# Batch 0 of a linear-attention kernel: nine tokens of k and v to a partition, one load queue, and v cast on chip

## The chip, the cores and the metric

The kernel runs on one NeuronCore of a Trainium2 chip. The metric is the device time of one execution in microseconds (us), as the median of several runs. A profiled execution gives a trace of every instruction of the five engines (PE is TensorE, DVE is VectorE, ACT is ScalarE, POOL is GpSimd, SP is SyncE) and of every DMA transfer.

## The reference

```python
# q, k, v: (8 batches, 8 heads, 576 tokens, 64), float32
q_s = softmax(q, axis=-1)                      # over the 64 features
k_s = softmax(k, axis=2)                       # over the 576 tokens
kv  = einsum('bhsd,bhse->bhde', k_s, v)
att = einsum('bhsd,bhde->bhse', q_s, kv)       # -> x: (8, 576, 512)
xn  = (x - mean(x)) / sqrt(var(x) + 1e-6) * g_ln
out = x + relu(xn @ w_ch1) @ w_ch2             # 512 -> 2048 -> 512
```

## The kernel before, in words

One pass over eight batches and a ninth group, C9, that holds the last 64 tokens of all batches. For each batch the kernel takes exponentials of q and k, forms k'v for each pair of heads, divides by k's sums, multiplies q's exponentials with it, normalises the rows, and runs the two large products with w1 and w2. TensorE's matmuls are written in a fixed order (`run` weaves a list of side steps into the list of matmuls by a position), and each engine works through its own instructions strictly in the order of the program. DMAs are issued in program order too: those of the queue SP by SyncE, those of GpSimd's queue by GpSimd between its computing instructions.

Everything that the change touches is the prologue, `first_batch()`, and its helpers, and one entry in the list of side steps of batch 0:

- q of batch 0 comes in four tokens to a partition (`T = 4`); k and v of batch 0 come in `T0 = 6` tokens to a partition, so that 576 tokens lie on `P0 = 96` partitions. Tokens 0 and 1 of q, then k in four pieces of two heads, are issued on SP's queue (L970, L980). A small copy on GpSimd (`gate`, L1004) waits for q's landing and holds back what GpSimd issues behind it: v in three pieces, cast to bf16 by the DMA itself (L1006), tokens 2 and 3 of q (L970), the first 512 columns of w1 in two halves (L1013), the other three blocks of w1 (L99), the first blocks of w2 (L103), and then the loads of batch 1.
- `warm(17)` and `warm(6)` are matmuls on zeros that keep TensorE busy (L867).
- `exp_qt` (L220) and `norm_q` (L274, L923) treat one token group of q; `eq_pT` (L928, L934 or L930) transposes it on TensorE and copies it from PSUM.
- `exp_k0` (L293) takes the exponentials of two heads of k. `z0_mm` (L306) sums them over the tokens by matmuls with a column of ones, `recip_z` (L314) takes the reciprocals.
- `kv0_mm` (L321, L322) multiplies a pair of heads with both heads of v as one 128 by 128 product, scales it and masks the two off-diagonal blocks (`diag`) with VectorE, which also sums the rows. From the sums ScalarE or VectorE writes a 128 by 128 weight `mbc` (L327, L331), which subtracts the mean.
- `xT_mm` (L342) forms the transposed, mean-free rows of x for tokens 0 and 1 from `kv_sb` and `mbc`, in two PSUM banks of two column blocks each; `xT_out` (L351 on VectorE for blocks 0 and 1, L353 on ScalarE for 2 and 3) scales them by the gain.
- The matmuls with w1 for batch 0 are L520 (`mm1_part`), first over m 0 to 3 for tokens 0 and 1. Between them `q0_rest(t)` does `z_q` (L940) and `po_mm` (L414) of tokens 2 and 3, `x_fast` and `x_normed` (L464, L475) finish these rows, and `xn_pT` transposes them (L928, L932).

The line that ends the first load group and the lines that order GpSimd's queue:

```python
        nc.gpsimd.tensor_copy(out=gate, in_=q0[:, 1, 0, 0:4])
        for h0, hn in ((0, 4), (4, 2), (6, 2)):
            nc.gpsimd.dma_start(
                v0[0:P0, h0 : h0 + hn].rearrange("p h t d -> p h (t d)"), src0(v, h0, hn)
            )
        for t in range(2, T):
            load_q0(t, 1, nc.gpsimd)
```

Of the kernel before, what the change touches and what calls it, by code (L numbers as in the profile page):

```python
# [12 lines left out]
FP32 = mybir.dt.float32  # L13
BF16 = mybir.dt.bfloat16
# [6 lines left out]
def kernel(  # L21
# [16 lines left out]
    nc = tc.nc  # L38
# [33 lines left out]
    ident = const.tile([P, P], BF16)  # L72
    eps_ln = const.tile([P, 1], FP32)
    gate = const.tile([P, 4], FP32)
    ones = const.tile([P, 1], BF16)
    junk = const.tile([P, P], BF16)
    scrap = const.tile([P, 512], BF16)
    bones = const.tile([P, 2], BF16)
    ones_w = const.tile([P, P], BF16)
    diag = const.tile([P, P], FP32)  # L80
    mbc = const.tile([P, NP, P], BF16)
# [204 lines left out]

    kvbox = {}

    def exp_k0(j):
        hs = slice(2 * j, 2 * j + 2)  # L290
        if j == 0:
            eks[0] = raw.tile([P, T0, H, D], BF16, tag="kt", name="ek0", bufs=1)
        nc.scalar.activation(  # L293
            eks[0][0:P0, :, hs, :].rearrange("p t h d -> p h t d"), raws[0][0][0:P0, hs], AF.Exp
        )

    def k0_mm(j, t):
        hs = slice(2 * j, 2 * j + 2)
        return eks[0][0:P0, t, hs, :], raws["v0"][0:P0, hs, t, :], P

    def z0_mm(j):

        if j == 0:
            kvbox["z0"] = mm_ps.tile([P, NP], FP32, tag="m", name="z0")
        for t in range(T0):
            nc.tensor.matmul(  # L306
                kvbox["z0"][:, j : j + 1], k0_mm(j, t)[0], ones[0:P0],
                start=(j == 0 and t == 0), stop=(t == T0 - 1), skip_group_check=True,
            )

    def recip_z():
        kvbox["rz"] = sml.tile([P, NP], FP32, tag="rzk", name="rzk")
        kvbox["sum"] = sml.tile([P, NP], FP32, tag="lnv", name="kvs")
        nc.vector.reciprocal(kvbox["rz"], kvbox["z0"])  # L314

    def kv0_mm(j):
        pool, tag = (att_ps, "a") if j < 2 else (mm_ps, "m")
        pkv = pool.tile([P, P], FP32, tag=tag, name="pkv")
        for t in range(T0):
            lhsT, rhs, w = k0_mm(j, t)  # L320
            nc.tensor.matmul(pkv[:, 0:w], lhsT, rhs, start=(t == 0), stop=(t == T0 - 1))  # L321
        nc.vector.scalar_tensor_tensor(  # L322
            kv_sb[:, 0, j, :], in0=pkv, scalar=kvbox["rz"][:, j : j + 1], in1=diag,
            op0=ALU.mult, op1=ALU.mult, accum_out=kvbox["sum"][:, j : j + 1],
        )
        if j < NP - 1:
            nc.scalar.activation(  # L327
                mbc[:, j], ones_w, AF.Copy, scale=kvbox["sum"][:, j : j + 1]
            )
        else:  # L330
            nc.vector.tensor_scalar_mul(  # L331
                out=mbc[:, j], in0=ones_w, scalar1=kvbox["sum"][:, j : j + 1]
            )

    def xT_mm(j, kh):

        if j == 0:
            pobox["T", kh] = mm_ps.tile([P, 2, 2, P], FP32, tag="m", name="pxT")
        ops = [(kv_sb[:, 0, j, :], j % 2)] if j // 2 == kh else []
        ops += [(mbc[:, j], i) for i in range(2)]  # L340
        for n, (lhsT, i) in enumerate(ops):
            nc.tensor.matmul(  # L342
                pobox["T", kh][:, i], lhsT, eqTs[0][:, 0:2, j, :],
                start=(j == 0 and n == 0), stop=(j == NP - 1 and n >= len(ops) - 2),
                skip_group_check=True,
            )

    def xT_out(i):
        dst, src = xnTs[0][:, 0:2, i, :], pobox["T", i // 2][:, i % 2]
        if i < 2:  # L350
# [4 lines left out]
    halves = (slice(0, 64), slice(64, P))  # L355

    def kv_pairs(b, ts=range(T + 1)):

# [501 lines left out]
        for _, fn in side[done:]:  # L860
            fn()

    def warm(n):

        w = mm_ps.tile([P, 4, P], FP32, tag="m", name="warm")
        for _ in range(n):
            nc.tensor.matmul(w, junk, junk[:, 0:4].to_broadcast([P, 4, P]), start=True, stop=True)  # L867

    def prep_fast(b):

# [74 lines left out]
    def eq_pT(c, t, eng):  # L945
        pe_T(eqTs[c], eqs[c][0][:, t].rearrange("p h d -> p (h d)"), t, eng)
# [10 lines left out]
    def first_batch():  # L957

        nc.scalar.preload_act_table_set("natural_log_exp_and_others")
        raws[0] = (  # L960
            mlp.tile([P, H, T0, D], FP32, tag="hT", name="kt0", bufs=1), None,
            raw.tile([P, H, T, D], FP32, tag="qt", name="qt"),
        )
        k0, _, q0 = raws[0]
        v0 = mlp.tile([P, H, T0, D], BF16, tag="hs", name="v0", bufs=1)
        raws["v0"] = v0

        def load_q0(t, tn, eng):
            ts = slice(t, t + tn)
            eng.dma_start(  # L970
                q0[:, :, ts],
                q[0, :, 0:SM, :].rearrange("h (p t) d -> p h t d", t=T)[:, :, ts],
            )

        def src0(x, h0, hn):
            return x[0, h0 : h0 + hn].rearrange("h (p t) d -> p h (t d)", t=T0)

        load_q0(0, 2, nc.sync)
        for h0 in range(0, H, 2):
            nc.sync.dma_start(  # L980
                k0[0:P0, h0 : h0 + 2].rearrange("p h t d -> p h (t d)"), src0(k, h0, 2)
            )
        raws["g"] = outp.tile([KO1, P], FP32, tag="ot", name="g_rows")
        nc.scalar.dma_start(
            raws["g"], bass.AP(moe_g_ln.tensor, moe_g_ln.offset, [[P, KO1], [1, P]])
        )
        nc.vector.memset(junk, 0.0)
        nc.vector.memset(eps_ln, 1e-6)
        nc.vector.memset(ones, 1.0)
# [3 lines left out]
        nc.vector.memset(ones_w, -1.0 / DM)  # L993
        nc.vector.memset(diag, 0.0)
        for ps in halves:
            nc.vector.memset(diag[ps, ps], 1.0)
        nc.vector.memset(kv_sb[:, 1:B], 0.0)
# [7 lines left out]
        for h0, hn in ((0, 4), (4, 2), (6, 2)):  # L1005
            nc.gpsimd.dma_start(  # L1006
                v0[0:P0, h0 : h0 + hn].rearrange("p h t d -> p h (t d)"), src0(v, h0, hn)
            )
        for t in range(2, T):
            load_q0(t, 1, nc.gpsimd)  # L1010
        for kh in range(2):
            ks = slice(2 * kh, 2 * kh + 2)
            nc.gpsimd.dma_start(w1_sb[:, ks, 0:512], w1_src[:, ks, 0:512])  # L1013
        for nb in range(1, 4):
            load_w1(nb)
        load_w2(0)
        load_w2(1)

        new_eq(0)
        start_x(0)  # L1020
        warm(17)
        for t in range(2):
            exp_qt(0, t)
            norm_q(0, t)
        eq_pT(0, 0, nc.vector)
        warm(6)
        eq_pT(0, 1, nc.vector)
        for j in range(NP):
            exp_k0(j)
            z0_mm(j)  # L1030
            if j == NP - 2:
                g_columns()
        recip_z()
        kv0_mm(0)
        kv0_mm(1)
        kv0_mm(2)
        xT_mm(0, 0)
        kv0_mm(3)
        exp_qt(0, 2)
        exp_qt(0, 3)  # L1040
        xT_mm(1, 0)
        xT_mm(2, 0)
        xT_mm(0, 1)
        xT_mm(3, 0)
        xT_out(0)
        xT_out(1)
        eq_pT(0, 2, nc.scalar)
        xT_mm(1, 1)
        xT_mm(2, 1)
        eq_pT(0, 3, nc.vector)  # L1050
        xT_mm(3, 1)
        xT_out(2)
        xT_out(3)

    def q0_rest(t):
        z_q(0, t)
# [35 lines left out]
    with tc.manual_schedule(  # L1092
# [11 lines left out]
        def po_x(c, t):  # L1104
            for i in range(NP):
# [85 lines left out]
```

## Time and profile before

| | |
|---|---|
| Median of 3 runs | 262.19 us (261.9 to 262.19) |
| Profiled execution: its own time | 262.09 us |
| Profiled execution: span of its instructions | 260.3 us, granted clock 1.000 |
| Outside the span | 1.8 us |
| TensorE busy | 253.9 us (98%) |
| VectorE, ScalarE, GpSimd busy | 223.1, 177.5, 103.2 us |
| DMA moved | 45.04 MB, mean 173 GB/s |

Times in the prologue are microseconds from the start of the span. In the views of the trace each line names an engine, the line of the kernel, the operation, and "output tile <- input tiles"; PEld is the loading of a matmul's weights, which overlaps the matmuls. A line number can be that of a helper: L520 is every matmul with w1 of batch 0 and some of batch 1. The chain of waits follows, from the last instruction backwards, what released each piece of work.

### The profile page before, as it was taken

The page shows a single profiled execution, that of the slowest core. Times are in us where ns is not written, and L with a number is a line of the kernel's source. Part 1 is how long each engine was busy: PE and PEld are TensorE (multiplying, and loading weights), DVE is VectorE, ACT ScalarE, POOL GpSimd, SP SyncE. Part 2 cuts the span into 40 slices and gives each one's busy share as a digit, 9 for nine tenths or more (in the row PEclk, how much of TensorE's full clock was granted, in tenths as well). Part 3 has the DMA queues.
Part 4 walks back from the last instruction along what each step waited for, and adds up shares of the span by engine and source line. Part 5 has one row for each costly group of instructions (what it writes and reads, how often), then busy time and mean ns, then how long its engine had stood idle before and what let it go on. Part 6 is the DMA issues. An engine that isn't in the chain of part 4 may idle for free.

```text
span 260.3 us, 7286 instructions
## 1 busy us (share of the span) xinstructions
PE 253.9 (98%) x2885; PEld 215.6 (83%) x2885; DVE 223.1 (86%) x542; ACT 177.5 (68%) x348; POOL 103.2 (40%) x160
## 2 busy tenths in 40 slices
PE   8899999999999999999999999999999999999993
PEld 3689755788888888888888988888889888888883
DVE  6768996989989998899889988998899889957873
ACT  4747790997988685888588858885788386647400
POOL 3953247410299409800980098008200900190000
PEclk9999999999999999999999999999999999999999
DMA  6999999988699995999699859989902630422014
GB/s 198 257 203 208 354 221 332 257 169 308 118 122 321 268 120 107 300 247 107 142 300 235 86 135 304 232 89 161 279 0 50 142 137 1 77 71 99 3 40 121
DMA packets 82618, 45.04 MB, mean 173 GB/s; under 512 B 58196, under 2 KB 79192, under 8 KB 82584
## 3 DMA queue, kind: packets, MB, share of 16 engines
q0 software_dynamic: 32464, 21.76, 45.8%
q1 hardware_dynamic: 49488, 22.29, 36.8%
q10 hardware_dynamic: 632, 0.53, 0.7%
q8 instruction: 22, 0.36, 0.6%
q14 instruction: 12, 0.10, 0.1%
HBM read 36.70 MB, written 9.44 MB: 177 GB/s over the span
## 4 chain that ended last, share of the span: by engine, by line
PE 92%; DMA 4%; POOL 2%; DVE 0%; issue 0%
PE ba L604 21%; PE bx L762 20%; PE bb L762 10%; PE ph L520 8%; PE bb L604 6%; PE be L604 5%; PE bc L604 5%; PE pc L556 5%; PE bc L762 5%; DMA w_raw<-in_moe_w_ch_dram 3%; PE pkv L371 2%; DMA qt<-in_q_dram 2%; PE po L403 2%; PE ptr L928 1%; PE po L414 1%; POOL v L1006 1%
## 5 line engine op out<-in xcount | busy, mean ns | idle before, releaser
L604 PEld LDWEIGHTS <-hs 128*128 128x128 bf16 x512 | 49.6, 98 | 6.0
L269 POOL TENSOR_TENSOR tq<-xnT 128x256 bf16<-128x256 bf16 x30 | 20.1, 671 | 85.3 <-PE bc L604 73.9
L762 PEld LDWEIGHTS <-w_raw 128*128 128x128 bf16 x480 | 46.7, 98 | 5.5
L604 PEld LDWEIGHTS <-hT 128*128 128x128 bf16 x392 | 37.6, 98 | 4.2
L762 PEld LDWEIGHTS <-w1g 128*128 128x128 bf16 x360 | 34.7, 98 | 4.3 <-issue 0.2
L762 PE MATMUL bx<-tq,w_raw 128*128 128x256 bf16 x240 | 31.3, 273 | 0.0
L604 PE MATMUL ba<-w_q,hs 128*128 128x256 bf16 x256 | 30.6, 273 | 0.0
L786 ACT COPY bc<-bx 128x512 f32<-128x512 f32 x30 | 16.7, 596 | 19.1 <-PE bx L762 19.1
L427 ACT ACTIVATE scrap<-x,mv 128x512 bf16<-128x512 bf16 x32 | 23.1, 723 | 4.6 <-DVE mv L457 4.4
L793 DVE TENSOR_TENSOR bb<-bx,s 128x512 f32<-128x512 f32 x30 | 19.5, 694 | 7.2 <-ACT s L790 4.5
L804 ACT ACTIVATE hT<-bb 128x512 bf16<-128x512 f32 x30 | 16.3, 595 | 9.3 <-PE bb L762 9.3
L804 ACT ACTIVATE hT<-bc 128x512 bf16<-128x512 f32 x30 | 16.5, 595 | 8.5 <-PE bc L762 8.5
L796 DVE TENSOR_TENSOR hT<-bx,s 128x512 bf16<-128x512 f32 x30 | 19.3, 684 | 3.2 <-PE bx L762 3.1
L587 DVE TENSOR_TENSOR hs<-hT 128x1024 bf16<-128x1024 bf16 x32 | 21.4, 672 | 0.5 <-ACT hT L804 0.5
L229 DVE TENSOR_REDUCE zq<-eq 128x16 f32<-128x1024 bf16 (+1 forms) x20 | 20.7, 1049 | 0.5 <-ACT eq L220 0.5
L269 POOL TENSOR_TENSOR tq<-xnT,tq 128x256 bf16<-128x256 bf16 x30 | 20.0, 669 | 1.1
L449 DVE SCALAR_TENSOR_TENSOR x<-po,rq 128x256 bf16<-128x256 f32 x48 | 17.5, 420 | 1.7 <-PE po L403 1.7
L790 ACT COPY s<-bb 128x512 f32<-128x512 f32 x30 | 16.6, 622 | 0.0
L804 ACT ACTIVATE hT<-bx 128x512 bf16<-128x512 f32 x30 | 16.4, 610 | 0.0
L762 PE MATMUL bx<-xnT,w1g 128*128 128x256 bf16 x120 | 16.2, 273 | 0.0
L762 PE MATMUL bx<-tq,w1g 128*128 128x256 bf16 x120 | 15.9, 272 | 0.0
L762 PE MATMUL bc<-xnT,w1g 128*128 128x256 bf16 x120 | 15.8, 273 | 0.0
(157 smaller groups left out, 535.0 us busy)
## 6 DMA issues: line engine op xcount, KB each, us to landing
out_dram<-ot POOLq DMA_DIRECT2D x30, 256.0 KB, 4.4
kt<-in_k_dram SPq DMA_DIRECT2D x5, 1024.0 KB, 11.6
qt<-in_q_dram SPq DMA_DIRECT2D x4, 1024.0 KB, 9.9
qt<-in_q_dram POOLq DMA_DIRECT2D x2, 1024.0 KB, 12.7
kt<-in_k_dram POOLq DMA_DIRECT2D x2, 1024.0 KB, 14.5
vm<-in_v_dram POOLq DMA_DIRECT2D x16, 128.0 KB, 12.4
qt<-in_q_dram SPq DMA_DIRECT2D x3, 512.0 KB, 5.7
w_raw<-in_moe_w_ch_dram POOLq DMA_DIRECT2D x3, 512.0 KB, 10.5
```

The costliest lines, as they stand in the source:

```text
L229: nc.vector.reduce_sum(eqs[c][1][:, ts], eqs[c][0][:, ts], axis=AX.X)
L269: nc.gpsimd.tensor_tensor(out=dst[:, t], in0=x[:, t], in1=y[:, t], op=ALU.subtract)
L427: nc.scalar.activation(scrap, x[:, t], AF.Square, bias=mv[:, t, 0:1], scale=-float(DM), accum_out=mv[:, t, 1:2],)
L449: nc.vector.scalar_tensor_tensor(x[:, t].rearrange("p (i two d) -> p i two d", two=2, d=D)[:, :, half], in0=pobox[c, t][half], scalar=1.0, ...
L520: nc.tensor.matmul(ph[:, m % 2, at : at + tn], (w1g if c else w1_sb)[:, ko, m * P : (m + 1) * P], xnTs[c][:, t0 : t0 + tn, ko, :], start=( ...
L587: nc.vector.tensor_tensor(out=dst, in0=x, in1=y, op=op)
L604: nc.tensor.matmul(hbox[bank][:, t, cs], lhsT, rhs[:, cs], start=first and (own or t == 0) and k == 0, stop=k == KH - 1, skip_group_check= ...
L762: nc.tensor.matmul(dst[:, q], lhsT, rhs, start=first and q == 0 and ko == 0, stop=ko == 1, skip_group_check=True)
L786: nc.scalar.copy(at[g, "c"], at[g, "x"])
L793: nc.vector.tensor_tensor(out=at[g, "b"], in0=at[g, "x"], in1=at[g, "s"], op=ALU.add)
L796: nc.vector.tensor_tensor(out=h_out(g, 1, 1), in0=at[g, "x"], in1=at[g, "s"], op=ALU.add)
L804: nc.scalar.activation(h_out(g, odd, half), at[g, name], AF.Relu)
```

## The change

- `T0` becomes 9. k and v of batch 0 lie on 128 partitions: 64 token groups of one head on partitions 0 to 63, the other head of the pair on 64 to 127, 2304 bytes in a row.
- SP's queue issues, in this order: q's tokens 0 and 1, four pieces of k, four pieces of v in fp32, and tokens 2 and 3 of q in four pieces of two heads. GpSimd's queue no longer carries v or q of batch 0. Its `gate` now waits for the last piece of k; behind it come the two halves of w1's first block, with two casts of v between them, blocks 1 and 2 of w1, and, at the end of the prologue, the copy `kv0_copy`, block 3 of w1 and the first blocks of w2.
- v is cast to bf16 by ScalarE (piece 0, parts of 2 and 3), GpSimd (piece 1, part of 3) and VectorE (part of 2), into a tile with a 65th column of ones, so that the sums of k's exponentials come out of the k'v product. `z0_mm` and `recip_z` go.
- k'v is formed for each head by itself: nine matmuls of 64 by 64 weights on partitions 0 to 63 and nine on 64 to 127, alternating, into a PSUM bank for each pair of heads. For two pairs at a time VectorE takes the reciprocals and scales one pair, ScalarE scales the other, both with row sums, and VectorE makes the mean column `kvm`; it is used as a weight by broadcasting it to 128 columns. GpSimd copies the result into `kv_sb`, which VectorE clears entirely beforehand.
- Each of the four column blocks of the transposed x has a PSUM bank of its own: 16 matmuls with the mean, 8 with the 64-row halves of `kvc`. `xT_out` uses VectorE for blocks 0 and 2, ScalarE for 1 and 3.
- The warming matmuls become three with fp32 and four with bf16 operands, and later one and two.
- The transposes of token 3 (`eq_pT(0, 3)`, with ScalarE's copy) move behind the first w1 matmuls, and `q0_rest(3)` one position back.

```diff
-    T0 = 6
-    P0 = S // T0
+    T0 = 9
...
+    def cast_v0(j, eng, ts=slice(0, T0)):
+        dst, src = raws["v0"][:, j, ts, 0:D], raws["v32"][:, j, ts]
...
+    def kv0_mm(j):
+        kvbox["kv0", j] = pkv = att_ps.tile([P, VW], FP32, tag="a", name="pkv")
+        for t in range(T0):
+            for ps in halves:
+                nc.tensor.matmul(
+                    pkv[ps], eks[0][ps, j, t], raws["v0"][ps, j, t],
+                    start=(t == 0), stop=(t == T0 - 1), skip_group_check=True,
+                )
+    def kv0_out(pair):
...
+        a, b = 2 * pair, 2 * pair + 1
+        nc.vector.reciprocal(rz[1], kvbox["kv0", b][:, D:])
+        nc.vector.reciprocal(rz[0], kvbox["kv0", a][:, D:])
+        nc.scalar.activation(
+            kvc[:, b], kvbox["kv0", b][:, 0:D], AF.Copy, scale=rz[1], accum_out=total[1]
+        )
+        nc.vector.scalar_tensor_tensor(
+            kvc[:, a], in0=kvbox["kv0", a][:, 0:D], scalar=rz[0], in1=ones_f,
+            op0=ALU.mult, op1=ALU.mult, accum_out=total[0],
+        )
+        js = slice(a, b + 1)
+        nc.vector.tensor_scalar_mul(
+            out=kvm[:, js], in0=kvbox["sum"][:, js], scalar1=-1.0 / DM
+        )
+    def kv0_copy():
+        for ps in halves:
+            nc.gpsimd.tensor_copy(out=kv_sb[ps, 0, :, ps], in_=kvc[ps])
...
-        load_q0(0, 2, nc.sync)
-        for h0 in range(0, H, 2):
-            nc.sync.dma_start(
-                k0[0:P0, h0 : h0 + 2].rearrange("p h t d -> p h (t d)"), src0(k, h0, 2)
-            )
+        load_q0(0, 2)
+        for dst, x in ((k0, k), (v32, v)):
+            for j in range(NP):
+                load_pair(dst, x, j)
+        for h0 in range(0, H, 2):
+            load_q0(2, 2, slice(h0, h0 + 2))
...
-        nc.gpsimd.tensor_copy(out=gate, in_=q0[:, 1, 0, 0:4])
...
+        nc.gpsimd.tensor_copy(out=gate, in_=k0[:, NP - 1, 0, 0:4])
+        load_w1_half(0)
+        cast_v0(1, nc.gpsimd)
+        load_w1_half(1)
+        cast_v0(3, nc.gpsimd, slice(0, 5))
+        for nb in range(1, 3):
+            load_w1(nb)
...
-        warm(17)
+        warm(3, junk_f)
+        warm(4)
         for t in range(2):
             exp_qt(0, t)
             norm_q(0, t)
         eq_pT(0, 0, nc.vector)
-        warm(6)
-        eq_pT(0, 1, nc.vector)
         for j in range(NP):
             exp_k0(j)
...
+        warm(1, junk_f)
+        warm(2)
+        eq_pT(0, 1, nc.vector)
+        cast_v0(0, nc.scalar)
+        g_columns()
         kv0_mm(0)
+        cast_v0(2, nc.vector, slice(0, 4))
+        cast_v0(2, nc.scalar, slice(4, T0))
         kv0_mm(1)
+        cast_v0(3, nc.scalar, slice(5, T0))
+        kv0_out(0)
         kv0_mm(2)
-        xT_mm(0, 0)
         kv0_mm(3)
+        for j in range(2):
+            xT_mean(j, 0)
+            xT_mean(j, 1)
+            xT_kv(j)
+        kv0_out(1)
         exp_qt(0, 2)
...
+        xT_mean(2, 0)
+        xT_mean(3, 0)
         xT_out(0)
         xT_out(1)
-        eq_pT(0, 2, nc.scalar)
...
+        xT_kv(2)
+        xT_kv(3)
+        eq_pT(0, 2, nc.vector)
+        xT_mean(2, 1)
+        xT_mean(3, 1)
+        exp_qt(0, 3)
         xT_out(2)
         xT_out(3)
+        kv0_copy()
+        load_w1(3)
+        load_w2(0)
+        load_w2(1)
...
-                (4, lambda: q0_rest(3)),
+                (3, lambda: eq_pT(0, 3, nc.scalar)),
+                (5, lambda: q0_rest(3)),
```

More of the change, by code (lines that the diff above doesn't have):

```diff
@@ L74 @@
     gate = const.tile([P, 4], FP32)
-    ones = const.tile([P, 1], BF16)
     junk = const.tile([P, P], BF16)
+    junk_f = const.tile([P, P], FP32)
     scrap = const.tile([P, 512], BF16)
     bones = const.tile([P, 2], BF16)
-    ones_w = const.tile([P, P], BF16)
-    diag = const.tile([P, P], FP32)
-    mbc = const.tile([P, NP, P], BF16)
+    ones_f = const.tile([P, D], FP32)
+    kvm = const.tile([P, NP], BF16)
+    kvc = const.tile([P, NP, D], BF16)
     g_one = const.tile([P, KO1], FP32)
@@ new lines, in kv0_mm @@
+    def kv0_mm(j):
[7 more added lines that the diff above has]
+    def kv0_out(pair):
+        if pair == 0:
+            kvbox["rz"] = sml.tile([P, NP], FP32, tag="rzk", name="rzk")
+            kvbox["sum"] = sml.tile([P, NP], FP32, tag="lnv", name="kvs")
+        rz, total = [
+            [kvbox[n][:, j : j + 1] for j in (2 * pair, 2 * pair + 1)] for n in ("rz", "sum")
+        ]
+        a, b = 2 * pair, 2 * pair + 1
+        nc.vector.reciprocal(rz[1], kvbox["kv0", b][:, D:])
+        nc.vector.reciprocal(rz[0], kvbox["kv0", a][:, D:])
@@ L311, in recip_z @@
[L311 to L333, printed above, removed]
@@ L345, in xT_mm, with xT_kv @@
                 skip_group_check=True,
             )
+    def xT_kv(j):
+        for ps in halves:
+            nc.tensor.matmul(
+                pobox["T", j][ps], kvc[ps, j], eqTs[0][ps, 0:2, j, :],
+                start=False, stop=False, skip_group_check=True,
+            )
     def xT_out(i):
-        dst, src = xnTs[0][:, 0:2, i, :], pobox["T", i // 2][:, i % 2]
-        if i < 2:
+        dst, src = xnTs[0][:, 0:2, i, :], pobox["T", i]
+        if i % 2 == 0:
             nc.vector.tensor_scalar_mul(out=dst, in0=src, scalar1=g_one[:, i : i + 1])
@@ L986, in first_batch @@
         )
+        nc.vector.memset(junk_f, 0.0)
         nc.vector.memset(junk, 0.0)
         nc.vector.memset(eps_ln, 1e-6)
-        nc.vector.memset(ones, 1.0)
         nc.vector.memset(bones, 0.0)
@@ L992, in first_batch @@
         nc.vector.memset(bones[64:P, 1:2], 1.0)
[L993 to L997, printed above, removed]
+        nc.vector.memset(ones_f, 1.0)
+        nc.vector.memset(raws["v0"][:, :, :, D:], 1.0)
+        nc.vector.memset(kv_sb, 0.0)
         nc.vector.memset(vr, 0.0)
```

85 lines of the change are left out of this document (28 added, 57 removed).

## The prediction

> **What bounds the kernel now.** I read the page first, then TensorE's waits, the chain of waits, the stages and the order of time of the first 20 us.
>
> The page's first table and TensorE's waits over the whole span (who waited for whom: total us, times, longest):
>
> ```profile
> PE 253.9 (98%) x2885; PEld 215.6 (83%) x2885; DVE 223.1 (86%) x542; ACT 177.5 (68%) x348; POOL 103.2 (40%) x160
> ...
> PE ptr L928 <- DVE eq L923: 1.0, 1, 1.0
> PE ph L520 <- DMA w_raw<-in_moe_w_ch_dram: 0.4, 1, 0.4
> ```
>
> TensorE is never idle long after 7.4 us; the last wait it has before its final matmul is 0.4 us for the second half of w1. So what the prologue costs is decided by when TensorE reaches the unbroken stretch of w1 matmuls, and everything behind it shifts with that moment. The chain of waits of the first 20 us shows the place (start us, us, what):
>
> ```profile
> 9.82 6.86 DMA w_raw<-in_moe_w_ch_dram
> 16.68 0.05 issue
> 16.72 0.61 PE ph L520 x4
> ...
> 18.44 0.95 PE ph L520 x16
> 19.39 0.34 PE ptr L928 x4
> 19.74 0.33 PE ph L520 x3
> ```
>
> The landing at 16.68 releases TensorE. The unbroken stretch (m 4 to 7, tokens 0 and 1) begins with a matmul at 19.57, shown here as 19.74. That is my mark. The order of time (start, length, engine, line, operation) gives its inputs:
>
> ```profile
> 6.11 0.82 ACT L293 ACTIVATE ek<-kt 96x768 bf16<-96x768 f32 x1
> 8.16 1.82 ACT L293 ACTIVATE ek<-kt 96x768 bf16<-96x768 f32 x2 [0.19 <-DMA kt<-in_k_dram]
> 11.83 0.50 PE L321 MATMUL pkv<-v,ek 96*128 96x128 bf16 x6
> 12.44 1.40 ACT L220 ACTIVATE eq<-qt 128x512 bf16<-128x512 f32 x2
> 14.62 0.60 PE L520 MATMUL ph<-xnT,w_raw 128*128 128x256 bf16 x4
> ```
>
> The trace's landing records put q at 5.03, k at 6.06, 7.11, 8.14 and 9.12, v at 10.18, 10.92 and 11.72, q's tokens 2 and 3 at 12.42 and 13.19, the w1 halves at 14.37 and 16.68. The last v releases the last k'v product, and 2.90 us after it (14.62) the first w1 matmul starts. The stages (us, busy by engine, granted clock, DMA share, GB/s) show that the DMA engines are full throughout:
>
> ```profile
> 3.00:4.50 1.50, 1.50 (x5) 0.56 (x4) 1.33 (x2) 0.00 (x0) 0.00 (x0) 1.00 1.13 357
> 5.50:7.50 2.00, 1.01 (x7) 0.28 (x5) 1.83 (x5) 1.80 (x4) 2.00 (x4) 1.00 1.08 285
> 8.50:10.50 2.00, 2.00 (x39) 1.59 (x38) 1.52 (x6) 1.35 (x2) 2.00 (x3) 1.00 1.31 200
> ```
>
> 357 GB/s is mostly q on 128 partitions, 285 is k on 96, 200 (as written, so 400 as read) is v being cast.
>
> **The change, part by part.** I walk to the mark in the new order; all times are us from the span's start.
>
> *k and v on 128 partitions.* An engine ends q at 4.50 at the latest. k's 1536-byte records then take 87 ns in the median on 96 partitions, but 65 ns (23.6 bytes/ns) in the first piece. q's 512 bytes take 27 ns with a pitch near 24 ns, and a 1024-byte load of a later batch 46 ns, on 128 partitions. For 2304 bytes I take 23.7 bytes/ns, 97 ns, since all clean rows on 128 partitions lie near it; the ends are 90 ns (the rate of 410 GB/s that q of batch 1 reaches) and 130 ns (k's 87 ns scaled by size). Each piece puts 8 records on an engine, 0.78 us, and k's last landing (9.12) trails its last record (8.43) by 0.69. So k lands at 6.0, 6.7, 7.5 and 8.3 (0.8 earlier at the end) and v at 9.1, 9.8, 10.6 and 11.37, against 11.72: 0.35 gained. At the ends v's last is 10.95 or 13.5.
>
> *Exponentials and casts.* ScalarE's line through 512 (0.62) and 768 elements (0.84) gives 0.68 for 576; the last exponential of k ends at 8.95 instead of 9.98, which no longer matters as v comes later. The casts of v are new work. Pieces 0 to 2 hide under the next piece's landing. Piece 3 does not: ScalarE's 4 tokens (256 elements) cost 0.40, GpSimd's 5 tokens about 0.46 by its copy of 1024 elements in 1.17; should its fp32 read cost double, 0.3 more.
>
> *GpSimd's order.* The gate now waits for k's last piece (8.3, was q's 5.03). Behind it are queued: w1's first half (issue 0.77), the cast of v's piece 1 (waits 9.8), w1's second half (issued 10.6 to 11.3), the cast of piece 3 (11.4 to 11.9), w1's blocks 1 and 2, the copy into kv_sb (waits for the last kvc), then w1 block 3 and w2. TensorE waits for that copy only at po of token 2, near 15.2; it is done by 14.4. The w1 issues stay ahead of the data, since the queue already holds over 2 us of transfers.
>
> *From v's last landing (11.37) to the first w1 matmul.* ScalarE's cast ends at +0.41, kvc(1) with its accumulator read at +0.68 (0.21 for the read, L485's), the mean column on VectorE at +0.85, TensorE starts xT at +0.90. VectorE's reciprocals of two pairs (0.18 each, by L314) and its product are done by then; the second pair's reach kvm at +1.80, under the first pair's matmuls. The removed z matmuls (24) and their reciprocal were not what ended last, and I credit nothing. xT is then bound by TensorE: 16 mean matmuls at 0.109, 4 pairs at 0.109 (two 64-row halves side by side, as L371 runs its halves), 4 transposes 0.23: 1.74 + 0.44 + 0.23 = 2.41. Together +3.31, so the first w1 matmul at 14.68. Unpaired halves would add 0.44.
>
> *From there to the mark.* Before, TensorE's work from 14.62 on is 8 matmuls, two z and po groups, and after the 0.4 wait 3.0 us up to 19.57: 4.5 net of the wait. The new order adds the transposes of token 3 (0.23) and a wait: z of token 3 is queued behind ScalarE's copy (0.58) of those transposes, about 0.38. Saved is the wait for w1, which should land near 15.6, with need at 16.1. The sum is 5.03 (rounding in the pitches), the mark 19.71, and +0.14 against 19.57.
>
> *q's tokens 2 and 3, the decisive cost.* They move from GpSimd's queue to the end of SP's, behind v: 64 records of 512 bytes an engine at 24 ns, 1.56 us. Alone, they end at 12.3 and land at 12.96. exp_qt(0, 2) then needs 0.62, the transposes, 4 mean matmuls: landing + 1.38 is the earliest first w1 matmul, and up to a landing of 13.3 nothing is late. Queued on ScalarE behind that exponential are xT_out(1) and exp_qt(0, 3); on TensorE, behind the transposes, the second half of xT and all of w1. But w1's first half is issued at 8.5, and its records (98 ns, pitch 82 ns) come on the other queue. In the trace v, issued from 5.20, shows its first record at 7.72, when the first engine has just finished k (7.71): what was already queued on SP went first. Later in this trace loads of SP and of GpSimd go one for one (59 and 60 records per 0.25 us at 113.5). I take it that most of q goes first and the last 8 to 12 records an engine alternate with w1: 8 to 12 times 82 ns, 0.65 to 1.0 us. The landing is then 13.6 to 13.9, the first w1 matmul 15.0 to 15.3, and the mark +0.5 to +0.75. I take +0.6.
>
> A page bears on this: the Trainium skill, DMA: Bandwidth & Descriptors, "Queues, rings and completion order", says each engine takes the queues with work in turn, packet by packet. By that rule w1 enters at once, and the rival below is the result; the trace agrees at 113.5 us and not at 7.7.
>
> *The rest.* Three fp32 and four bf16 warming matmuls replace 17; the only clue to their length is the 0.43 us of a cold bf16 one. Anything up to 1.3 us too long hides under the 1.0 us wait at 6.4 to 7.4 and the gap before k'v; a saving buys nothing. VectorE's set-up writes lose ones_w and diag (0.17 + 0.17 + 0.28) and gain 0.22 on kv_sb and some 0.4 for junk_f, ones_f and v's ones: it must be free at 5.66, and is. kv0 in 18 small matmuls costs under 0.4 a pair, one after each cast. Behind the mark nothing changes; data is 0.2 to 0.6 earlier, TensorE later, so no wait for w1 or w2 arises.
>
> The sum: 262.09 (profiled; the median shown is 262.19) + 0.6 is 262.7, or 262.8 against the median.
>
> **The rivals.**
>
> 1. *Faster: landings and a shorter chain* (0.29). If records of 2304 bytes go at 90 ns, v's last lands at 10.95 and q's at 12.4, both early enough: the first w1 matmul comes at 14.26 (-0.28 at the mark). If the copy behind z of token 3 also stays hidden, another 0.38 goes: 261.4 to 261.9. It decides as soon as the first w1 matmul is before about 14.0 or that wait is absent. For it: k's first piece at full rate. Against it: it needs both.
>
> 2. *Slower: w1 alternates with all of q's tokens 2 and 3* (0.20). If w1 enters at 11.0 (2.5 us after its issue, as v did), each of q's records waits for one of w1's: 16 get through before, the other 48 take 32 turns of 106 ns beside both halves of w1 and 16 more beside block 1, to 16.1; landing 16.8, the first w1 matmul 18.2, the mark +3.6: 265.7. It costs anything from a landing after 13.3 on; with half of it, 263.9.
>
> 3. *Slower: large records are no quicker on 128 partitions* (0.08). At 130 ns v's last lands at 13.5: +2.2, 264.4.
>
> 4. *TensorE falls back to half clock* (0.03). Between 9.3 and 12.3 it now works some 1.2 us. Half speed over 3.4 us, the time the clock needed at the start (matmuls of 0.43 until 4.3), costs 1.7: 264.5. The trace has no such fall after an idle 1.0 us.
>
> The forecast keeps 0.40: first w1 matmul between 14.7 and 15.6, 262.2 to 263.2.
>
> **How the numbers follow.** 0.2% (0.52 us) is about what a measurement of this kernel can tell from no change. The forecast is split about evenly by that bound, 0.18 within and 0.22 beyond. Rival 1 gives 0.25 beyond and 0.04 within; rivals 2 to 4 give 0.29 beyond on the slow side and 0.02 within. So: faster 0.25, same 0.18 + 0.04 + 0.02 = 0.24, slower 0.22 + 0.29 = 0.51. The range leaves out a tenth at each end: rival 1's better part and the worse half of rival 2, 261.3 to 265.2.
>
> **What would show it.** Right: k's last landing near 8.3, v's near 11.4, q's tokens 2 and 3 near 13.7, the first w1 matmul at 15.0 to 15.3, no wait for w1's second half, z of token 3 waiting 0.4 for ScalarE. Wrong: exp_qt(0, 2) not waiting for a landing, or waiting beyond 15; v's last landing before 11 or after 12.

## The result, and the profile after

The changed kernel takes 263.31 us (median of 8 runs, 263.07 to 265.07), the kernel before beside it 262.06 (8 runs): a ratio of 1.0061, 95% interval 1.0038 to 1.0084. It is slower, by twice the forecast 0.6 us. The profiled execution took 264.21 us, with a span of 262.4 and a mean granted clock of 0.991.

First the page's table of busy time, then TensorE's waits over the whole span (who waited for whom: total us, times, longest):

```profile
PE 255.7 (97%) x2904; PEld 215.4 (82%) x2904; DVE 222.7 (85%) x541; ACT 177.7 (68%) x352; POOL 101.1 (39%) x159
```

```profile
...
PE pkv L307 <- ACT kvc L323: 1.0, 1, 1.0
PE zs L948 <- ACT eqT L938: 0.2, 1, 0.2
```

The 0.4 us wait for w1 is gone. In its place TensorE waits once for 1.0 us, with a k'v product (L307) waiting for ScalarE's kvc (L323). The prediction has no such wait. (A wait of 1.1 us that stands ahead of it in the answer is that of the first warming matmul for its zeros, long before q lands.) The chain of the first 22 us:

```profile
5.03 5.54 DMA v<-in_v_dram
...
10.60 0.41 ACT v L298
11.00 0.31 ACT kvc L323 x2
...
11.36 0.77 PE pkv L307 x34
12.13 0.97 PE pxT L344 x4
13.10 0.35 PE pxT L353 x2
...
16.78 0.44 PE ph L528 x4
```

Between v's last landing (10.57) and the mean matmuls stand a cast, kvc, and then 0.77 us of k'v. Four mean matmuls and the step to what follows them take 0.97 here, where I had put 0.44 for four. The stages say why (us, busy by engine, granted clock, DMA share, GB/s), first of this execution, then, for the last of these stages, of the same kernel run again:

```profile
5.50:7.50 2.00, 1.79 (x11) 0.76 (x9) 1.93 (x5) 2.00 (x4) 0.00 (x0) 1.00 1.04 403
8.50:10.50 2.00, 1.70 (x44) 1.29 (x43) 1.30 (x7) 1.05 (x2) 1.51 (x3) 1.00 1.06 382
12.50:15.00 2.50, 2.50 (x13) 1.05 (x12) 0.40 (x3) 0.79 (x3) 2.10 (x5) 0.50 1.17 175
```

```profile
12.50:15.00 2.50, 2.50 (x23) 1.36 (x24) 1.18 (x6) 1.31 (x5) 2.10 (x5) 1.00 1.23 186
```

k now arrives at 403 GB/s where it had 285. But in the trace's record of the clock it is 0.50 from 12.06 to 15.48, while in the other execution of the very same kernel it stays at 1.00. The loss therefore has two parts: a longer chain, and, in 3 of the 8 runs (mean clock 0.990 or 0.991, the profiled one among them), the fall of the clock. From here on, a run with a fall means one whose mean clock is 0.994 or less; where its fall lies is known only of the executions with a profile. The runs without a fall have a median of 263.19, those with one 264.27.

From the order of time come the two ends of q's tokens 2 and 3:

```profile
12.67 0.62 ACT L219 ACTIVATE eq<-qt 128x512 bf16<-128x512 f32 x1
18.66 0.25 PE L948 MATMUL zs<-bones,eqT 128*128 128x2 bf16 x4 [0.24 <-ACT eqT L938]
```

The exponential of token 2 names no landing as what it waited for; it runs behind kvc's accumulator read. The landing records put q's last at 12.10 (12.73 in the run again, where that exponential also follows the read at once), not 13.7.

This table puts the stretches side by side (us, starts taken from the order of time; the landings from the trace's landing records; "mark" as in the prediction). The last two kernels are described below.

| | before | predicted | run again, no fall | halves in one group | final version |
|---|---|---|---|---|---|
| q's first landing to v's last | 6.69 | 6.34 | 5.74 | 5.77 | 5.94 |
| v's last landing to the first w1 matmul | 2.90 | 3.63 to 3.93 | 4.58 | 4.26 | 3.83 |
| first w1 matmul to the mark | 4.95 | 5.03 | 5.00 | 5.06 | 4.78 |
| sum | 14.54 | 15.0 to 15.3 | 15.32 | 15.09 | 14.55 |

Of the 1.06 us between the spans of before and of the run again (260.31 and 261.37), the sum of the table has 0.78; q's first landing came 0.16 later in that execution, and the rest lies behind the mark.

### The profile page after: what moved, and what is told of

Read it like the earlier page. It is cut to its first block, busy times and chain, and to the rows that moved or that the text cites. A ratio compares the mean times of both kernels' runs of the same rounds, so it can differ in the third digit from the quotient of the medians.

```text
span 262.4 us, 7342 instructions
## 1 busy us (share of the span) xinstructions
PE 255.7 (97%) x2904; PEld 215.4 (82%) x2904; DVE 222.7 (85%) x541; ACT 177.7 (68%) x352; POOL 101.1 (39%) x159
## 4 chain that ended last, share of the span: by engine, by line
PE 94%; DMA 4%; ACT 0%; DVE 0%; SPq 0%; issue 0%
PE ba L612 21%; PE bx L770 20%; PE bb L770 10%; PE ph L528 8%; PE bb L612 6%; PE be L612 5%; PE bc L612 5%; PE pc L564 5%; PE bc L770 5%; DMA v<-in_v_dram 2%; PE pkv L379 2%; PE po L411 2%; DMA qt<-in_q_dram 1%; PE pxT L344 1%; PE ptr L936 1%; PE po L422 1%
## 6 DMA issues: line engine op xcount, KB each, us to landing
vm<-in_v_dram POOLq DMA_DIRECT2D x16, 128.0 KB, 12.3
```

## The experiments

My first theory after the result: two PSUM banks for four pairs make pair 2 wait, the broadcast weights of the mean are slow, and a clock that falls in some runs adds the rest. The rivals were chance differences between executions, and the new warming matmuls. The median of before beside a run lies between 262.1 and 262.6, as the runs were taken on several chips; each ratio is to the runs of before on the same chip.

**1. The changed kernel again**, and **2. the old warming matmuls**, all bf16:

```diff
-        warm(3, junk_f)
-        warm(4)
+        warm(17)
...
-        warm(1, junk_f)
-        warm(2)
+        warm(6)
```

> The changed kernel once more, unaltered, for a second profile. Its eight runs lie in two groups: 264.2 to 265.1 us with a mean granted clock near 0.990, and 263.1 to 263.4 with 0.997 to 1.000. Theory A (the granted TensorE clock falls to half for 3.41 us in the prologue, at 12.06 in the first profile, because TensorE had too little work in the 3.4 us before): a profile of the lower group shows a fall that is shorter, later, or beside the matmuls that end last. Theory B (the PSUM banks of k'v: pairs 2 and 3 wait 1.0 us for the banks of pairs 0 and 1): both groups show the wait of 1.0 us at 11.36, and that wait is what the lower group still loses against before (about +1.1 us).

> The warming matmuls of the kernel before (17 and 6 in bf16) in place of 3 fp32 + 4 and 1 fp32 + 2. If it is the form of the warming that lets the clock rise late (5.24 instead of 4.22) and fall: no fall, time as with the fillers, 261.9 to 262.4. If it is the gaps between the k'v products (theory A as I hold it): the fall stays, 263 to 264.5. Theory B: 263.1 to 263.4, same.

Again: 263.52 (262.88 to 265.32, 12 runs), ratio 1.0051 [1.0031, 1.0070]; 4 of 12 runs have a clock of 0.990 or 0.991 and a median of 264.63, the other 8 one of 263.12. Old warming: 263.5 (9 runs), 1.0059 [1.0029, 1.0089], one run in nine with a fall. The loss repeats, and the warming matmuls are not its cause. In these two sets of runs a fall costs about 1.1 to 1.5 us. Of the 32 runs of before on the same chip none fell. The kernel before is not free of falls, though: on the other chips of the later runs, 4 of its 47 have a mean clock of 0.990 to 0.994 and take 264.0 to 266.35 us, and none of these has a profile. The order of time of the execution without a fall:

```profile
11.72 0.77 PE L307 MATMUL pkv<-v,ek 64*64 64x65 bf16 x36 [1.02 <-ACT kvc L323]
...
12.42 0.61 PE L344 MATMUL pxT<-eqT,kvm 128*128 128x256 bf16 x4
...
12.96 0.30 PE L353 MATMUL pxT<-eqT,kvc 64*64 64x256 bf16 x2
...
13.19 0.61 PE L344 MATMUL pxT<-eqT,kvm 128*128 128x256 bf16 x4
...
15.51 0.60 PE L528 MATMUL ph<-xnT,w_raw 128*128 128x256 bf16 x4
```

From the first mean matmul to the first w1 matmul it is 3.09 us; I had counted 2.41.

**3. Banks of their own for pairs 2 and 3**, and **4. warming matmuls in the gaps of k'v**. The changed kernel takes all four banks of k'v from a pool with two, so pairs 2 and 3 use those of pairs 0 and 1 again; the kernel before took pairs 2 and 3 from the other pool, and the change dropped that:

```diff
-        pkv = att_ps.tile([P, VW], FP32, tag="a", name="pkv")
+        pkv = (att_ps if j < 2 else mm_ps).tile(
+            [P, VW], FP32, tag="a" if j < 2 else "m", name="pkv")
```

```diff
         kv0_mm(0)
+        warm(1)
...
         kv0_out(0)
+        warm(4)
         kv0_mm(2)
```

> Pairs 2 and 3 of k'v get banks of the other pool, so that they no longer wait for pairs 0 and 1 to be read. Theory B: k'v of pair 2 starts near 10.4 and of pair 3 near 11.1, the mean matmuls at 11.4 instead of 12.06, time lower by 0.6 to 1.0 us in each group: 262.3 to 262.6. Theory A: the wait moves, the clock falls all the same (the same matmuls in the same window), and at half clock the 2.4 us of matmuls with x still end late: 262.5 to 264, the two groups stay.

> One warming matmul behind pair 0 of k'v and four in front of pair 2 (0.21 us each at full clock, in gaps of 0.37 and 1.1 us). Theory A: no fall of the clock in the prologue, mean clock 1.000 in all runs, the spread gone; the first w1 matmul near 14.6 instead of 16.6, time 261.9 to 262.4. Theory B: no gain at all, 263.1 to 263.4 at best, since the wait for the banks stays; if the clock was fallen anyway, the fillers take 1.7 us at half clock and cost some tenths.

Banks: 263.03 (12 runs), 1.0028 [1.0011, 1.0045], one fall; without it 263.01, so the 262.3 to 262.6 expected did not come. TensorE's waits in its profile, and the piece of its chain behind v's last landing:

```profile
PE pkv L308 <- POOL v L300: 0.7, 2, 0.4
...
PE pxT L345 <- DVE rzk L322: 0.2, 1, 0.2
```

```profile
11.06 0.41 ACT v L298
11.47 0.31 ACT kvc L324 x2
...
11.80 0.42 DVE kvm L332
12.22 0.07 DVE rzk L322
12.29 1.02 PE pxT L345 x4
```

The wait for kvc is gone, but the mean column, which also needs ScalarE's kvc behind its cast of v, is late next, and it takes VectorE 0.42 us where I had put 0.17: the first mean matmul starts 1.22 us after the last cast of v begins (11.06 to 12.28), where it was 1.46 (10.96 to 12.42). So the 1.0 us wait was worth about a quarter of a microsecond. Filling the gaps instead (263.2, 12 runs, 1.0040 [1.0023, 1.0057]) leaves the runs without a fall at 263.19, and has one fall in 12 where the kernel again had four. The banks alone, without any filler, also had one in 12, so these counts do not show that fillers of this number help; the 261.9 to 262.4 that went with the theory of the clock did not come.

**5. Dense mean weights in place of the broadcast column:**

```diff
-    kvm = const.tile([P, NP], BF16)
+    kvm = scrap.rearrange("p (j n) -> p j n", j=NP)
...
-            out=kvm[:, js], in0=kvbox["sum"][:, js], scalar1=-1.0 / DM
+            out=kvm[:, js], in0=kvbox["sum"][:, js].to_broadcast([P, 2, P]), scalar1=-1.0 / DM
...
-                pobox["T", i], kvm[:, j : j + 1].to_broadcast([P, P]),
+                pobox["T", i], kvm[:, j],
```

> The mean column is written by VectorE as a dense 128x128 weight for each pair (256 elements for two pairs instead of 2) in place of the broadcast column. Theory (the broadcast weight makes each of the 16 mean matmuls 0.135 us, not 0.109, worth 16 x 0.027 = 0.43 us): four of them take about 0.44 to 0.46 us instead of 0.54, the weight write takes 0.1 to 0.2 us longer and delays the first of them by that, the stretch from the first mean matmul to the first w1 matmul shrinks from 3.18 to about 2.75, and the time falls by 0.25 to 0.35 us, to about 263.1 where the changed kernel is 263.4. Rival (0.135 is the spacing that comes from the alternating PSUM banks, not from the weights): four still take 0.54 and the time rises by 0.1 to 0.2.

264.34 (6 runs), 1.0078 [1.0050, 1.0105], three falls; without them 263.29. This part of my theory falls:

```profile
13.11 0.61 PE L344 MATMUL pxT<-eqT,scrap 128*128 128x256 bf16 x4
13.65 0.30 PE L353 MATMUL pxT<-eqT,kvc 64*64 64x256 bf16 x2
13.88 0.61 PE L344 MATMUL pxT<-eqT,scrap 128*128 128x256 bf16 x4
```

The theory gave about 263.1, its rival a rise. The pitches are the same to the hundredth as with the broadcast column. The single records show what I had read wrongly in the groups: mean matmuls start at 13.110, 13.230, 13.339 and 13.448, so they run at 0.109; the two halves start at 13.651 and 13.654, so they do run side by side; but the step into the halves is 0.203 where 0.109 was due, and the step out of them 0.226. A pass from 128-row to 64-row weights costs 0.09 us, the way back 0.12 (0.09 to the transposes), and the written order does this three times: about 0.6 us. The trace of before has such steps too, where k'v of batch 1 (L371) follows larger matmuls:

```profile
41.34 0.59 PE L556 MATMUL pc<-w_sb,hT 128*128 128x512 bf16 x2
41.86 0.32 PE L371 MATMUL pkv<-vm,ek 128*64 128x65 bf16 x8
```

The second of the two L556 starts at 41.552, and at their pitch of 0.216 L371 was due at 41.77; its first record starts at 41.861. Later in that trace a 256-column matmul of L604 is followed six times by matmuls with 64 by 64 weights (L403), each time after 0.202 or 0.203 us, as in the new kernel.

**6. The halves in one group.** The new theory, tested by order alone:

```diff
         for j in range(2):
             xT_mean(j, 0)
             xT_mean(j, 1)
-            xT_kv(j)
...
         xT_mean(3, 0)
+        for j in range(NP):
+            xT_kv(j)
         xT_out(0)
         xT_out(1)
-        xT_kv(2)
-        xT_kv(3)
```

> All eight 64-row halves of kvc stand in one group behind 12 of the mean matmuls, instead of three groups between them; the same matmuls, nothing else changed. Theory (the mean matmuls run at 0.109 us and the halves side by side, but each pass from 128-row to 64-row matmuls and back costs 0.09 and 0.12 us, three times): the stretch from the first mean matmul to the first w1 matmul falls from 3.09 to 2.67 us, by 0.42, perhaps 0.05 to 0.1 less for a wait on the second pair's mean column, and the median falls from 263.4 to about 263.0. Rival (the 0.21 us stands beside work of other engines that ends as late, the exponential of token 2 or the copy of the transposes): the first w1 matmul moves by under 0.15 and the time stays.

262.99 (12 runs), 1.0025 [0.9999, 1.0050], three falls; without them 262.83, against 263.12 for the changed kernel again. Over the runs of before without a fall on each chip that is +0.45 and +0.82. The intervals of the two ratios overlap, so it is the trace that decides.

```profile
11.99 1.61 PE L344 MATMUL pxT<-eqT,kvm 128*128 128x256 bf16 x12
...
13.53 0.62 PE L353 MATMUL pxT<-eqT,kvc 64*64 64x256 bf16 x8
...
14.76 0.60 PE L528 MATMUL ph<-xnT,w_raw 128*128 128x256 bf16 x4
```

The stretch is 2.77 us instead of 3.09; 2.67 was expected, and part of the difference is a short wait for the second pair's mean column (written 12.76 to 12.93, due at 12.87). With two of the three rounds taken out by order alone, the stretch shrank by 0.32 of the 0.42 expected: the passes are shown to be the main missing term of xT.

**7. w1 issued early**, with the gate on q again:

```diff
-        nc.gpsimd.tensor_copy(out=gate, in_=k0[:, NP - 1, 0, 0:4])
+        nc.gpsimd.tensor_copy(out=gate, in_=q0[:, 1, 0, 0:4])
```

> GpSimd's gate waits for q's tokens 0 and 1 again (near 5), so w1's first half is issued near 5.2 and not near 7.9. Theory (what SP's queue already holds goes first; w1's records began at 11.1 only because they came behind it): w1's first record still shows at 10.5 to 11.2, k, v and q land as before within 0.2 us, and the time stays within 0.2 us of the changed kernel. Rival (a transfer on GpSimd's queue starts 2.5 to 3.2 us after its issue whatever SP holds, and then takes turns with SP): w1's records start near 8.0, v's last landing moves from 10.6 to about 12, and the time rises by 1.0 to 1.5 us.

266.22 (265.71 to 266.53, 4 runs), 1.0149 [1.0135, 1.0163]; all four fell. The rival holds; the rise is larger than its 1.0 to 1.5, as all four also fell, and without a fall the same loads take 264.89 (experiment 9). Its stages, and the piece of its chain that ends with v:

```profile
8.50:10.50 2.00, 1.30 (x26) 1.00 (x25) 0.94 (x5) 1.13 (x2) 0.42 (x1) 1.00 1.10 315
10.50:12.50 2.00, 0.48 (x18) 0.36 (x18) 0.73 (x5) 0.46 (x1) 0.91 (x2) 1.00 1.14 287
```

```profile
5.04 7.56 DMA v<-in_v_dram
```

w1's first half, issued at 4.83, shows its records from about 9.0 on, although SP's queue still holds two pieces of v, and q, that were issued before it could start. From there the two queues go about one for one (41 records of w1 and 52 of v in the half microsecond from 9.0, 44 and 38 in the next), and v's last landing moves to 12.60. By the Trainium skill, "DMA: Bandwidth & Descriptors", "Queues, rings and completion order", the engines take the queues in turn, and here the trace agrees. So w1 behind k is not an ornament of the change: in the changed kernel its records begin only at 11.16, 3.3 us after the issue at 7.86, when 157 of q's 1024 records are left. What keeps q free of w1 is that delay, not the order of the queues.

**8 to 10. The clock.** The second group of warming matmuls left out; then, on the kernel with early w1, eleven warming matmuls of full size in the two gaps of k'v, and the same eleven with 32 by 32 weights, by a helper of their own (the last two also with the gate on q of experiment 7):

```diff
-        warm(1, junk_f)
-        warm(2)
```

```diff
         kv0_mm(0)
+        warm(2)
...
         kv0_out(0)
+        warm(9)
         kv0_mm(2)
```

```diff
+    def warm32(n):
...
+            nc.tensor.matmul(
+                w[0:32], junk[0:32, 0:32], junk[0:32, 0:4].to_broadcast([32, 4, P]),
+                start=True, stop=True,
+            )
...
         kv0_mm(0)
+        warm32(2)
...
         kv0_out(0)
+        warm32(9)
         kv0_mm(2)
```

> The second group of warming matmuls (one fp32, two bf16, near 7.5 to 8.5) is left out; they feed nothing. Theory (the granted clock falls to half for 3.4 us when TensorE has done too little in the microseconds before about 12, and that fall, not the chain, makes the runs of the changed kernel that end above 264): nearly all runs show the lower mean clock of 0.99 and end at 264.2 to 265.4; the profile shows 0.5 from about 12 on for 3.4 us, or an earlier fall. Rival (the fall is chance and not tied to how busy TensorE is): a third of the runs or fewer fall, and the median stays at 263.4.

> The kernel with w1 issued early again, plus 2 and 9 warming matmuls of 128 by 128 weights and 512 columns behind the k'v of pairs 0 and 1, where TensorE waits for v and kvc. Theory (a 3.41 us window in which TensorE uses less than about a quarter of its array-time, counted by rows times columns of the weights, is followed by 3.41 us at half clock; the kernel with early w1 had 0.14 in the window before its fall, and all four of its runs had a mean clock of 0.986 to 0.993): the window rises to about 0.7, no run shows a mean clock under 0.995, and the median falls from 266.2 to about 265.0. Rival (the fall is not decided by TensorE's work): the clocks stay at 0.99 and the time at 266.

> The same eleven warming matmuls in the same places and with the same 512 columns each, but with 32 by 32 weights, a sixteenth of the array. Theory (work is counted by the part of the array that it uses): the window stays under 0.2, most runs still show a mean clock of 0.986 to 0.993, and the median stays near 266.2. Rival (what counts is only whether TensorE streams): as with the full weights, no run falls and the median is near 265.0.

| | median, runs | ratio to before | runs with a fall |
|---|---|---|---|
| fewer warming matmuls | 264.39, 7 | 1.0073 [1.0047, 1.0099] | 4 of 7 |
| early w1 | 266.22, 4 | 1.0149 [1.0135, 1.0163] | 4 of 4 |
| early w1, 11 full fillers | 264.89, 7 | 1.0086 [1.0055, 1.0117] | 0 of 7 |
| early w1, 11 fillers of 32 by 32 | 266.36, 6 | 1.0139 [1.0087, 1.0190] | 4 of 6 |

The nine fillers ahead of pair 2 take the same 2.13 us in both last kernels, so TensorE is equally busy; what differs is how much of the array they use. With the full ones no run of 7 fell, with the small ones 4 of 6 did, on the same chip. The two runs of the small ones without a fall (264.78, 264.87) are as quick as those with the full ones. With fewer warming matmuls 4 of 7 fell, after 4 of 12; that is not nearly all, as expected, and with so few runs it is not shown to be more.

**11. A first combination** (banks, dense weights, another split of v's last cast, four fillers) and **12. the final version**, which drops the dense weights and one filler and adds the one group and the later z:

> The corrections together: PSUM banks of their own for pairs 2 and 3 of k'v, dense mean weights, the last piece of v cast by GpSimd (six tokens) and VectorE (three) so that ScalarE's kvc(1) does not stand behind a cast, and four more warming matmuls in TensorE's gaps between the k'v groups. Theory (the loss is made of the wait for kvc before pair 2's k'v, 0.3 to 0.5 net, the broadcast weights 0.3 net, the clock's fall in some runs; the halves of xT that do not run side by side, 0.4, stay): no wait for kvc, xT starts near v's last landing + 1.1 (was + 1.56), the first w1 matmul comes near 14.7 to 15.0, the mark near 19.8, no fall of the clock, and the time is 262.0 to 262.6, within 0.2% of the kernel before. Rival (something behind the first w1 matmul is now what bounds, such as z of token 3 or kv_sb's copy): the mark does not move with the first w1 matmul and the time stays above 262.8.

The final version has the banks of 3, the group of 6, and these edits (the first in `kv0_out`):

```diff
+        if pair == 0:
+            cast_v0(3, nc.vector, slice(6, T0))
         js = slice(a, b + 1)
...
-        cast_v0(3, nc.gpsimd, slice(0, 5))
+        cast_v0(3, nc.gpsimd, slice(0, 6))
...
         kv0_mm(0)
+        warm(1)
...
         kv0_mm(1)
-        cast_v0(3, nc.scalar, slice(5, T0))
+        warm(2)
         kv0_out(0)
...
-                (5, lambda: q0_rest(3)),
+                (6, lambda: q0_rest(3)),
```

> The corrections that the runs bear out, together: banks of their own for the k'v of pairs 2 and 3, the halves of kvc in one group, the last piece of v cast by GpSimd (six tokens) and VectorE (three) so that ScalarE's kvc(1) does not stand behind a cast, three full-array warming matmuls in the gaps of the k'v, and the z of token 3 one position later, so that ScalarE's copy is hidden. Theory (the loss of the changed kernel is the chain from v's last landing to the first w1 matmul, the wait of z, and the clock's fall): the first w1 matmul comes 3.8 us after v's last landing (5.1 in the changed kernel run again, 4.3 with the halves grouped), z of token 3 does not wait, no run has a mean clock under 0.995, and the median is 261.9 to 262.4, about that of the kernel before, or up to 0.2% faster. Rival (the work behind the first w1 matmul takes back what comes sooner: w1's second half, kv_sb's copy, the rows of token 3): the mark follows by less than half and the median stays above 262.7.

The first combination: 263.35 (5 runs), 1.0038 [1.0025, 1.0051], no fall. Its xT starts 1.36 us after v's landing (11.26 to 12.62) and not 1.1, since one of my fillers stands ahead of pair 3's k'v, and the three rounds of passes are still in it; the 262.0 to 262.6 expected did not come. The final version: 262.76 (262.15 to 264.10, 12 runs) beside 262.55 of before (17 runs), ratio 1.0001 [0.9974, 1.0028], no fall in 12 runs. Two of those 17 have a fall; the other 15 have a median of 262.45.

```profile
11.68 1.63 PE L347 MATMUL pxT<-eqT,kvm 128*128 128x256 bf16 x12
...
13.24 0.62 PE L356 MATMUL pxT<-eqT,kvc 64*64 64x256 bf16 x8
...
14.47 0.60 PE L531 MATMUL ph<-xnT,w_raw 128*128 128x256 bf16 x4
```

The first w1 matmul comes 3.83 us after v's last landing, as expected, z of token 3 does not wait, and the sum of the table is that of before. The median missed the 261.9 to 262.4 expected, and lies above the 262.7 of the rival although the mark did follow. The earlier landing of v, 0.75 us, is then spent entirely on a chain that is still 0.93 longer than the old one; the remaining 0.17 comes from the stretch behind it, 4.78 instead of 4.95. No version was shown to beat the kernel before; beside its runs without a fall the final one is 0.2 to 0.3 us behind.

## Why the prediction was right, and where not

The direction held, and the time lay inside the range, but the loss was twice the forecast: +0.6 forecast, +1.25 between the medians, +1.1 without the falls. That the sum from q's landing to the mark came to 15.32, beside my 15.0 to 15.3, is partly luck. The loss I forecast was nearly all the cost of q's tokens 2 and 3, 0.3 to 0.6 beyond a sum of +0.14, and that cost did not occur. The transfers were 0.60 quicker than I had put them. The chain from v's last landing to the first w1 matmul, 3.31 in my sum without q, took 4.58, and this 1.27 made up for both.

- *q's tokens 2 and 3, "the decisive cost"*: this step failed. They landed at 12.10 (12.73 in the run again; my case "alone" said 12.96, my forecast 13.6 to 13.9), and nothing waited for them. w1's first record came at 11.16, near the 11.0 of my rival of alternation, but 867 of q's 1024 records were through by then. So w1 met the last 157, 9.8 to an engine, where I had said 8 to 12; that count was right, but for another reason than mine. By q's rate just before (about 160 records in 0.25 us) I estimate that it held them up by some 0.4 us. I took from v's first record that what is already queued on SP goes first; experiment 7 shows that it does not, and that I had taken the delay between an issue and its first record for an order.
- *k and v on 128 partitions*: I put them too slow. The last of k came at 7.68 (8.3 said), of v at 10.57 (11.37 said). Part of that is this execution, in which q landed at 4.64 and not at 5.03. A record took 93 ns (97 said), and v's last landing trailed its last record by 0.31, where I had 0.69 from k. Over the profiles of kernels with the same loads v's last landing lies between 10.50 and 11.62, so 11.37 is near the late end.
- *From v's landing to the mean matmuls*: +1.49 where I had +0.90. The failed part is that the k'v of pairs 2 and 3 was taken to be done one after each cast. The text ahead of the prediction gives each pair a PSUM bank, but there are two for the four pairs, and pair 2 must wait until kvc of pairs 0 and 1 has been read out of them. The banks alone gave back only 0.24, since the mean column comes from the same kvc and took 0.42 where I had 0.17; taking ScalarE's cast out of kvc's way as well brought it to 1.04 (final version, 10.64 to 11.68). There the mean column took 0.16; why it took 0.42 in the other runs stays open.
- *xT, 2.41*: measured 3.09. The 0.109 for mean matmuls and for a pair of halves were right; missing was about 0.6 for the six passes between 128 and 64 rows. "Unpaired halves would add 0.44" named the wrong cause. The Trainium skill, "TensorEngine Tiling (Array Packing)", "Tiling Modes", says that changing the tiling mode drains TensorE; the trace agrees, with 0.09 and 0.12 us. The trace of before had the same steps (experiment 5), one of them at the edge of L371, the very row that I leaned on (its halves have 128 rows and 64 columns); they were there to be weighed and I did not.
- *From there to the mark, 5.03*: 5.00 measured. z of token 3 waits 0.24 behind ScalarE's copy where I had about 0.38. w1's second half landed at 14.82 with no wait, as said.
- *Exponentials, casts, GpSimd's order, warming*: as said; ScalarE's kvc and its read ended 0.74 after the landing (0.68 said).
- *The rivals*: large records took 93 ns, between rival 1's 90 and my 97, but the shorter chain that rival needs did not come. Rival 4, half clock over 3.4 us, had 0.03 and happened in 7 of 20 runs of this kernel. I had counted TensorE's busy time between 9.3 and 12.3 and seen no fall after an idle 1.0 us before; the trace of before does not show it. By the count of array use below, no 3.41 us of that trace behind the clock's rise and before its last matmuls has less than 0.45, while the changed kernel's window has 0.23.

## What to carry to other kernels

Before replacing large matmuls by small ones on parts of the array, count the passes between the two kinds in the written order (0.09 and 0.12 us each here) and put the small ones together, and ask how much of the array is used while the clock is being judged. When a step is split over fewer PSUM banks than it has pieces, the reader of the first piece is on the path of the third. A saving in transfers (here 0.75 us) is kept only if the chain behind the last landing gets no longer than that.

## What the runs showed of the hardware

- The clock's falls came at 12.06, 12.26 and 14.20 in three profiles, each lasting 3.41 us, and 6.83, 6.83 and 10.24 us (two, two and three times 3.41) after the clock's rise. I counted for each 3.41 us window the columns of its matmuls at 0.109 us for 256, times the part of the 128 by 128 array that their weights fill (an estimate from the records, of which some may be missing). The windows before the three falls have 0.23, 0.18 and 0.14; the lowest without a fall have 0.23, 0.26, 0.27 and 0.27. Without the weighting the falls (0.66, 0.62, 0.47) and the others (down to 0.40) mix. This and experiments 9 and 10 speak for a bound of about a quarter of the array's time; with a window of 0.23 on either side it is no sharper than that. It does not explain the 4 falls in 47 runs of the kernel before, whose trace has no window as low; these stay open. The Trainium skill, "TensorE: Matmul & The Clock Gate", "HAM oscillation — how this bites in real kernels", puts the danger at idle gaps over some 3.4 us; in the changed kernel's window, 8.65 to 12.06, TensorE was never idle for longer than the 0.96 us before pair 2's k'v, and the clock fell all the same.
- That the same kernel falls in some executions and not in others would follow if the windows count from the clock's rise, which came 3.96 to 7.05 us after the start in the profiles: in the two executions of the changed kernel it came at 5.24 (window 8.65 to 12.06, 0.23, a fall) and 5.95 (9.36 to 12.77, 0.27, none). Two executions fit this; they do not show it.
- The first record of a load issued by GpSimd came 2.5 us (v, before), 3.3 us and 4.1 us (w1) after the issue began. What sets the difference stays open.
